# Turning the attention output on the crossbar from batch 2 on, with loads in strict order and more staging

## The chip, the cores and the metric

The kernel runs on one core of one Trainium2 chip. The metric is the device time of one execution in microseconds (us), as the median of several runs of the whole program. Runs are marked fast or slow by their time against the fastest of the same kernel.

Some words that return: in this kernel **TensorE** (PE in the profile) multiplies, **VectorE** (DVE) and **ScalarE** (ACT) work on what it leaves in the memory PSUM, **GpSimd** (POOL) does casts and masks, and **SyncE** (SP) does little but issue DMA transfers (copies between memories). The plan gives each engine one list of instructions. `SPq` in a profile line is SyncE's queue: the time from the start of a DMA-issuing instruction to the moment when the next one may follow. "Crossbar" is here the transpose that a DMA does on its way from SBUF, the on-chip memory, to SBUF.

## The reference, cut to what matters

```
# q, k, v: (8 batches, 8 heads, 576 rows, 64), float32
scores = q @ k^T / 8
scores = where(row // 64 >= column // 64, scores, -1e9)     # block-causal
a = softmax(scores) @ v
x = a.transpose(0, 2, 1, 3).reshape(8*576, 8*64)             # 4608 x 512
h = x @ w_in                                                # 512 -> 2048
out = (h / (1 + exp(-beta * h))) @ w_out                     # 2048 -> 512
```

The feed-forward part needs x with its 512 features on the partitions, so the output of every head pair must be transposed (turned) once: 576 rows of 128 features become 128 partitions of 576 columns. With 8 batches of 4 pairs there are 32 such turns. Q and K of every pair are turned too, to feed the scores.

## The kernel before

The program is first planned and then emitted. Every operation is given to a list scheduler with an assumed length, its dependences, its buffer slots and a priority; the scheduler fixes one order for each of the five engines, and this order is what runs.

```
def schedule(self):                     # cut
    ...
    for e in engs:                      # PE, ACT, DVE, POOL, SP
        if eng_free[e] > now + 1e-9: continue
        for o in pool:                  # operations whose inputs are ready
            ...
            k = (o.prio, o.idx) if e in ("PE",) else (o.prio, o.ready, o.idx)
            ...
        start = now
        eng_free[e] = start + o.dur     # o.dur: the assumed length
        order[e].append(o)              # this order is emitted as it stands
```

Q and K of batches 2 to 7 come in groups of five loads on SyncE (two pairs at a time), are cast to bf16 on GpSimd, and are turned on the crossbar, again by SyncE (cut):

```
z = [g.dma_start(ST[ts.slot][:, i, :, :], src[b, h, 128*i:128*i+128, :]...) for i in range(4)]
z.append(g.dma_start(ST[ts.slot][0:64, 4, :, :], src[b, h, 512:576, :]...))
ld[nm, u] = ld[nm, u + 1] = P.op("SP", 5 * 400, fl, deps=szero, tiles=[ts], xfer=3200, prio=u, ...)
...
def ft(g, e, ...):
    return [g.dma_start_transpose(dst[td.slot][:].rearrange("c (t n) -> c t n", n=128),
                                  nat[tn.slot][:, 0:640])]
cps[nm] = P.op("SP", 1000, ft, deps=[o], tiles=[td, tn], xfer=1500, prio=-1, ...)
```

V comes in six loads per batch, also on SyncE, with a priority that lets it run far ahead; the stores of the result are SyncE's as well. After the attention product and its normalization into the tile xq, TensorE turns the pair and VectorE copies it to x^T, which is kept whole:

```
NE = 3                                  # slots of the exp tiles E
NS = 5                                  # staging slots ST
xq = [sb(f"xq{i}", [128, 5, 128], bf16) for i in range(2)]
xT = sb("xT", [128, 4, NROWS], bf16)    # 4608 columns
...
def fx(g, e, tx=tx, px=px):
    for i in range(5):
        r = 128 if i < 4 else 64
        z = g.transpose(PSb[:, px.slot, 128*i:128*i+r], xq[tx.slot][0:r, i, :], identB[0:r, 0:r])
    return z
xp = P.op("PE", 5 * 57, fx, deps=nrm, tiles=[tx, px], ...)
def fy(g, e, px=px, c=c, b=b):
    return g.tensor_copy(xT[:, c, S*b:S*(b+1)], PSb[:, px.slot, 0:576])
xt.append(P.op("DVE", 425, fy, deps=[xp], tiles=[px], prio=0))
```

The softmax here doesn't subtract the row's maximum and nothing guards it: scores larger than these inputs give would overflow.

## Time and profile before

| what | kernel before |
|---|---|
| median of 4 runs | 389.77 us (389.38 to 391.21) |
| profiled span, mean granted TensorE clock | 389.1 us, 0.947 |
| TensorE / VectorE / ScalarE / GpSimd busy | 349.6 / 168.4 / 209.4 / 96.6 us |
| turns of the attention output on TensorE | 160 instructions (32 pairs of 5) |
| crossbar transposes | 48 (Q and K of 24 pairs) |
| end of the last K transpose on SyncE's queue | 268.3 us |
| feed-forward matmuls after the last attention product | 460 |

These are the busy digits of the page of the kernel before: the span is cut into 40 equal slices (9.7 us each), a digit is the busy share in tenths, and in PEclk it is the granted TensorE clock in tenths.

```profile
PE   3875969999895789999999999999999999999986
PEclk9985779999999569999999999999999999999999
DMA  7989979897998799698967798413001102002002
```

After the uneven first six slices the reader is to see one dent in the PE row, slices 13 to 15 (the hole at 119 to 143 us, with the clock down to 0.5), nearly full digits from then on, and DMA engines that are heavily used until some 240 us and then nearly free. The last attention product runs at 284 us; from there to the end it is feed-forward work alone.

### The profile page before, as it was taken

The numbers are of one execution on the slowest core, as the hardware profiler recorded it, in microseconds if no ns is written. First come the engines' busy times: TensorE is split into PE (matmuls) and PEld (weight loads), VectorE is DVE, ScalarE is ACT, GpSimd is POOL, SyncE is SP. The second block draws the span as 40 slices with busy tenths as digits, with TensorE's granted clock in tenths as the row PEclk, the third lists the DMA queues.
The fourth block names the chain that finished last, engine by engine and source line by source line (L and its number), as shares of the span: only waits on it lengthen the run. The fifth ranks groups of instructions, "written<-read, shape, count | busy, mean of one in ns | idle before, by whom it ended". The sixth has DMA issues, their size and how long they took to land.

```text
span 389.1 us, 6936 instructions
## 1 busy us (share of the span) xinstructions
PE 349.6 (90%) x2709; PEld 176.3 (45%) x2753; DVE 168.4 (43%) x347; ACT 209.4 (54%) x306; POOL 96.6 (25%) x204
## 2 busy tenths in 40 slices
PE   3875969999895789999999999999999999999986
PEld 1552435444452445445545555454554444444432
DVE  5753585217520437413752266512670460550710
ACT  3641648127813458456883788817861551751721
POOL 4390263432202522244153353401100000000000
PEclk9985779999999569999999999999999999999999
DMA  7989979897998799698967798413001102002002
GB/s 173 194 113 229 225 123 180 182 211 168 240 199 176 186 178 199 135 184 205 189 144 167 185 170 144 91 54 89 2 1 56 54 1 83 27 0 83 27 27 81
DMA packets 140384, 50.27 MB, mean 129 GB/s; under 512 B 128560, under 2 KB 135744, under 8 KB 140352
## 3 DMA queue, kind: packets, MB, share of 16 engines
q1 hardware_dynamic: 135744, 45.64, 54.1%
q0 software_dynamic: 4608, 4.20, 7.3%
q8 instruction: 21, 0.34, 0.4%
q14 instruction: 11, 0.09, 0.1%
HBM read 36.71 MB, written 9.44 MB: 119 GB/s over the span
## 4 chain that ended last, share of the span: by engine, by line
PE 68%; DMA 8%; SPq 8%; ACT 7%; DVE 6%; issue 2%; POOL 0%
PE PS L603 29%; PE PS L627 28%; PE PS L546 5%; ACT E L511 5%; PE PS L504 4%; SPq L396 3%; DMA ST<-in_q_dram 3%; ACT th L611 2%; DVE gT L615 2%; DMA KT<-Kn 2%; PE PS L573 2%; SPq L464 2%; DMA w_in<-in_moe_w_in_dram 1%; SPq L400 1%; DMA out_dram<-ost 1%
## 5 line engine op out<-in xcount | busy, mean ns | idle before, releaser
L603 PE MATMUL PS<-xT,w_in 128*128 128x512 bf16 x550 | 135.3, 394 | 6.6 <-DVE xT L579 2.7
L615 DVE SCALAR_TENSOR_TENSOR gT<-th,PS 128x512 bf16<-128x512 f32 x144 | 97.5, 685 | 91.2 <-ACT th L611 91.0
L627 PE MATMUL PS<-w_out,gT 128*128 128x512 bf16 x558 | 125.1, 379 | 4.4 <-DVE gT L615 2.2
L611 ACT ACTIVATE th<-PS,beta 128x512 f32<-128x512 f32 x144 | 98.0, 698 | 42.3 <-PE PS L603 41.1
L511 ACT ACTIVATE E<-PS 128x1024 bf16<-128x1024 f32 x96 | 94.6, 1035 | 40.1 <-PE PS L504 39.9
L627 PEld LDWEIGHTS PS<-w_out,gT 128*128 128x128 bf16 x576 | 54.9, 98 | 68.4 <-DVE gT L615 3.4
L603 PEld LDWEIGHTS PS<-xT,w_in 128*128 128x128 bf16 x576 | 54.0, 101 | 68.9 <-issue 7.8
L638 ACT ACTIVATE ost<-PS 128x512 f32<-128x512 f32 x33 | 19.7, 597 | 94.0 <-PE PS L627 92.2
L504 PE MATMUL PS<-QT,KT 64*128 64x448 bf16 (+5 forms) x384 | 40.9, 303 | 6.6 <-ACT E L511 3.1
L546 PE MATMUL PS<-Vn,E 128*128 128x65 bf16 x960 | 38.0, 201 | 5.5 <-POOL E L519 3.5
L546 PEld LDWEIGHTS PS<-Vn,E 128*128 128x128 bf16 x960 | 35.3, 102 | 12.7 <-POOL E L519 6.6
L579 DVE COPY xT<-PS 128x576 bf16<-128x576 bf16 x32 | 14.5, 454 | 44.1 <-PE PS L573 44.1
L556 DVE RECIPROCAL inv<-PS 128x5 f32<-128x5 f32 x64 | 8.3, 173 | 55.5 <-PE PS L546 55.1
L517 POOL MEMSET E<- 64x128 bf16 x64 | 13.6, 212 | 64.8 <-ACT E L511 60.7
L504 PEld LDWEIGHTS PS<-QT,KT 64*128 64x128 bf16 (+1 forms) x384 | 14.8, 99 | 31.4 <-issue 10.5
L564 DVE TENSOR_TENSOR xq<-PS,inv 128x320 bf16<-128x320 f32 x64 | 28.5, 486 | 0.0
L410 POOL CAST Vn<-Vs 128x2560 bf16<-128x2560 f32 (+2 forms) x9 | 18.8, 2085 | 24.0 <-DMA Vs<-in_v_dram 22.1
L477 POOL CAST Qn<-ST 128x640 bf16<-128x640 f32 x24 | 17.3, 722 | 29.4 <-DMA QT<-Qn 26.7
L477 POOL CAST Kn<-ST 128x640 bf16<-128x640 f32 x24 | 17.3, 723 | 22.0 <-DMA KT<-Kn 19.4
L519 POOL MEMSET E<- 64x256 bf16 x32 | 10.1, 316 | 43.0 <-ACT E L511 42.5
L573 PE MATMUL PS<-identB,xq 128*128 128x128 bf16 (+1 forms) x160 | 17.5, 224 | 1.5 <-DVE xq L564 1.4
L573 PEld LDWEIGHTS PS<-identB,xq 128*128 128x128 bf16 (+1 forms) x160 | 12.5, 100 | 11.8 <-DVE xq L564 2.1
(31 smaller groups left out, 71.3 us busy)
## 6 DMA issues: line engine op xcount, KB each, us to landing
out_dram<-ost SPq DMA_DIRECT2D x36, 256.0 KB, 2.3
Vs<-in_v_dram SPq DMA_DIRECT2D x28, 256.0 KB, 4.6
ST<-in_q_dram SPq DMA_DIRECT2D x48, 128.0 KB, 2.8
ST<-in_k_dram SPq DMA_DIRECT2D x48, 128.0 KB, 2.7
ST<-in_q_dram SPq DMA_DIRECT2D x8, 288.0 KB, 4.2
ST<-in_k_dram SPq DMA_DIRECT2D x8, 288.0 KB, 4.4
w_in<-in_moe_w_in_dram POOLq DMA_DIRECT2D x16, 128.0 KB, 5.7
w_out<-in_moe_w_out_dram POOLq DMA_DIRECT2D x16, 128.0 KB, 4.3
```

Source lines behind the costliest of these rows:

```text
L410: return g.tensor_copy(Vn[t.slot][:, :, h0:h1, 0:64], Vs[ts.slot][:, :, h0:h1, :])
L477: return g.tensor_copy(nat[tn.slot][:, 0:640].rearrange("p (t h d) -> p t h d", t=5, h=2), ST[ts.slot][:, :, a:a + 2, :])
L504: z = g.matmul(o, KT[tk.slot][r, 128 * t:128 * t + m], QT[tq.slot][r, q0:q1])
L511: return g.activation(E3[te.slot][:, g0, :, :], PS[:, ps.slot:ps.slot + 2, :], ACT.Exp, scale=0.125)
L546: z = g.matmul(o, eblk(te, t, i, h), Vn[Tv.slot][:, t, 2 * c + h, 0:65], start=(t == 0), stop=(t == i))
L564: return g.tensor_tensor(xq[tx.slot][:, :, 64 * w:64 * w + 64], a, x, ALU.mult)
L573: z = g.transpose(PSb[:, px.slot, 128 * i:128 * i + r], xq[tx.slot][0:r, i, :], identB[0:r, 0:r])
L603: z = g.matmul(PS[:, ph.slot, :], w_in[:, c, 128 * j:128 * j + 128], xT[:, c, row:row + RC], start=(c == 0), stop=(c == 3))
L611: return g.activation(th[tt.slot][:], PS[:, ph.slot, :], ACT.Tanh, scale=beta[:, j:j + 1])
L615: return g.scalar_tensor_tensor(out=gT[tg.slot][:, j, :], in0=th[tt.slot][:], scalar=1.0, in1=PS[:, ph.slot, :], op0=ALU.add, op1=ALU.mult)
L627: z = g.matmul(PS[:, po.slot, :], gT[tg.slot][:, j, 128 * w:128 * w + 128], w_out[:, j, :], start=(j == 0), stop=(j == NJ - 1))
L638: return g.activation(ost[to.slot][:], PS[:, po.slot, :], ACT.Copy, scale=0.5)
```

## The change

The intent: TensorE is the bound, so take work off it. For batches 2 to 7 the turn of the attention output goes to the crossbar. The free crossbar has its price in the queue, so the change also puts the loads into strict order of use with a limited backlog, so that V no longer runs ahead of Q and K. It keeps x^T in a ring of 2560 columns instead of 4608, and spends the memory won on staging (7 slots instead of 5) and on exp tiles (4 instead of 3). Some assumed lengths of the plan are raised as well. The core of the diff:

```
-        NE = 3
-        NS = 5
+        NE = 4
+        NS = 7
+        RX = 5 * RC                                  # 2560
-        xT = sb("xT", [128, 4, NROWS], bf16)
+        xT = sb("xT", [128, 4, RX], bf16)
 ...
-                o = ld["V", b, h0] = P.op("SP", 6 * 400, fv, ..., prio=... 4 * b + 0.5 - 3 * (b > 1), ...)
+                o = ld["V", b, h0] = P.op("SP", 3000 + 2200 * n, fv, ..., prio=... 4 * b + 0.5, ...)
 ...
+        def pieces(b):                               # split at 512 rows, and where the ring wraps
+            z = []
+            for t0, n in ((0, 512), (512, 64)):
+                x0 = (S * b + t0) % RX
+                m = min(n, RX - x0)
+                z.append((t0, m, x0))
+                if m < n:
+                    z.append((t0 + m, n - m, 0))
+            return z
 ...
-  ... P.op("SP", 5 * 400, fl, ...)
+  ... P.op("SP", 5 * 570, fl, ...)
-  cps[nm] = P.op("SP", 1000, ft, ..., xfer=1500, ...)
+  cps[nm] = P.op("SP", 1280, ft, ..., xfer=800, ...)
 ...
+            if b >= 2:
+                def fy(g, e, tx=tx, c=c, b=b):
+                    z = []
+                    for t0, n, x0 in pieces(b):
+                        ...
+                        z.append(g.dma_start_transpose(xT[:, c, x0:x0+n].rearrange("c (t n) -> c t n", n=m), i))
+                    return z
+                n = len(pieces(b))
+                xt.append(P.op("SP", 400 + 300 * n + 700, fy, deps=nrm, tiles=[tx], xfer=1100, prio=-1, ...))
+                continue
 ...
+        for x, y in zip(seq, seq[1:]):               # seq: all loads of Q, K and V in order of use
+            y.after = x
+        for o in seq:
+            o.lazy = True                            # no load while the assumed backlog is over 4 us
 ...
+            # a crossbar turn into a slot of the ring waits for the matmuls that read it (hs)
+                        xt[4 * b + c].deps += hs
```

A turn is two DMA instructions for most batches and three where the ring wraps (batch 4): 52 for 24 pairs. The plan assumes 1.7 us for a turn of two.

## The prediction

> **What bounds the kernel now.** I read in this order: the table of stretches (busy time and clock), the waits, the chain, the groups, the issuing queue in order of time. The stretches (after the times: each engine's busy us with instructions, granted TensorE clock, DMA share, GB/s):
>
> ```profile
> 28.00:44.00 16.00, 11.91 (x70) 5.56 (x72) 6.55 (x13) 3.44 (x5) 2.68 (x4) 0.57 1.14 224
> 44.00:62.00 18.00, 14.92 (x105) 6.59 (x106) 12.81 (x22) 11.70 (x18) 10.52 (x22) 0.81 0.91 161
> 62.00:119.00 57.00, 53.75 (x440) 27.03 (x444) 22.52 (x51) 26.45 (x39) 14.46 (x24) 1.00 0.94 197
> 119.00:143.00 24.00, 15.91 (x155) 9.12 (x155) 6.32 (x17) 10.53 (x15) 9.50 (x17) 0.64 0.82 190
> 143.00:289.00 146.00, 141.07 (x1317) 74.32 (x1339) 69.76 (x160) 101.80 (x151) 43.54 (x92) 1.00 0.67 132
> ```
>
> The first engine column is TensorE. From 143 us on it works 141 of 146 us at full clock: **TensorE bounds most of the kernel**, so an instruction taken off it there is time saved. Two stretches are different: up to 62 us the DMA engines are full (share 0.9 to 1.1) and TensorE waits at a reduced clock; and 119 to 143 is a hole, with 8 us idle and clock 0.64. The chain of waits says what made the hole:
>
> ```profile
> 118.56 0.63 SPq L467 DMA_DIRECT2D ST<-in_k_dram  x1
> 119.24 1.29 SPq L483 DMA_TRANSPOSE KT<-Kn  x1
> 120.58 2.23 SPq L464 DMA_DIRECT2D ST<-in_q_dram  x4
> 122.85 0.62 SPq L467 DMA_DIRECT2D ST<-in_q_dram  x1
> 123.52 1.30 SPq L483 DMA_TRANSPOSE QT<-Qn  x1
> 124.86 1.28 SPq L483 DMA_TRANSPOSE KT<-Kn  x1
> ```
>
> These are lines of the SyncE queue's time order. The queue issues without a gap from 62 to 126 us; TensorE waits for K transposes that stand behind loads for later use (V of batches 3, 4 and 5 went out ahead of Q and K of batches 2 and 3). The groups that matter:
>
> ```profile
> L573 PE MATMUL PS<-identB,xq 128*128 128x128 bf16 (+1 forms) x160 | 17.5, 224 | 1.5 <-DVE xq L564 1.4
> L579 DVE COPY xT<-PS 128x576 bf16<-128x576 bf16 x32 | 14.5, 454 | 44.1 <-PE PS L573 44.1
> QT<-Qn SPq DMA_TRANSPOSE x24, 2.9
> KT<-Kn SPq DMA_TRANSPOSE x24, 2.7
> ```
>
> The first two are what the change replaces for 24 of 32 head pairs, the last two what it adds more of: 48 crossbar transposes exist, each 2.7 to 2.9 us from issue to landing.
>
> **What the Trainium skill says.** "TensorE: Matmul & The Clock Gate", Part 4, says a TensorE transpose goes to PSUM and needs a copy after it; the trace agrees (L573, then L579). Its Part 1 says the array falls to half clock after about 3.4 us of idleness and needs as long a busy stretch to recover; here the 5 us windows hold 0.50 between 30 and 40 us, and 3 us windows 0.50 from 127 to 142 us, after scattered short waits. "DMA: Bandwidth & Descriptors", "Issuing engine by pattern", allows a transpose only from SyncE or ScalarE; here all are SyncE's, so new ones join the queue that made the hole. "VectorE: DVE Perf Modes", "The three transpose paths", gives 390 ns on TensorE against 1309 ns by crossbar for 128x128. The trace is kinder to both: 224 ns of overlapped busy time, and 2.8 us to land five blocks.
>
> **Part by part.**
>
> TensorE and VectorE. 24 pairs lose 5 transposes each. Their price is not 5 x 224 ns, as they overlap: in the time order the start of such a group lies 0.32 to 0.45 us before the start of the next, so 24 x 0.39 = **9.4 us off TensorE**. VectorE loses 24 x 0.45 = 11 us of copies; it is 43% busy, so this gives nothing by itself. Eight early copies are split in two pieces by the ring; small.
>
> The hole. With loads in strict order, Q and K of the first pairs of batch 2 and then V go first, and V of batch 3 comes after Q of the second pairs. In 119 to 143 TensorE does three attention products, four score groups, two transposes and 7 matmuls: about 9 us at full clock. So **up to 14 us** can be had.
>
> Early part. w_in and w_out are gated as before. The order lets 16 instead of 8 matmuls of the first chunk run before the next Q transpose, and drops a 3.9 us wait of the queue for a staging slot; but with four E buffers the w_out issues on GpSimd now stand behind the masks of two later pairs. I take 2 us gained on TensorE (first chunk done at 84 instead of 86) and the first batch-2 load at 64 instead of 62.
>
> Issuing queue. Durations from its rows, with gaps: a group of five Q or K loads 2.93 us (2.23 + 0.62 + gaps), the six V loads 4.96 (3.12 + 1.77), a crossbar transpose 1.32 (1.28). The x^T turn of a pair is two instructions, 512 and 64 columns (three where the ring wraps), 576 instead of 640 columns: 1.2 us if time goes with columns, 1.7 if half of the 1.28 is fixed per instruction. I take 1.45, an estimate. From the first batch-2 load to the last K transpose: 24 x 2.93 = 70, 6 x 4.96 = 30, 48 x 1.32 = 63, some 20 stores x 0.6 = 12, 21 new turns x 1.45 = 31: **206 us**, against 172 of the same kinds before, where the queue took 62 to 268 and so was idle or held for 32 us of it.
>
> DMA engines. From 242 to 250 us little but transposes run, at shares 0.64 and 0.48: about 0.75 us of all 16 engines each. 24 x 0.7 = 17 us more in a stretch where the share falls from about 0.9: it fits, with no room to spare.
>
> The sum. In the changed order of instructions 616 feed-forward matmuls and 24 pairs stand between the end of the first chunk and the last attention product, then 408 matmuls. A matmul costs 0.22 us (448 in 98.5 us from 287.4 to 385.9), a pair without its turn 2.05 (attention product 0.95 to 1.0, twelve score matmuls 1.05). If TensorE never waits: 84 + 616 x 0.22 + 24 x 2.05 = 269, + 408 x 0.22 = 359, + 3 to the end = **362**. If the queue sets the pace: 64 + 206 + 3 (stores of the first chunk hold it once) = 273 for the last K; the K of the second last pair, which the order asks for first, lands at about 274; then 48 matmuls and two pairs, 15 us, + 90 + 3 = **382**. Per pair the queue needs 206/24 = 8.6 us and TensorE 185/24 = 7.7, so after using up its lead the queue is the slower one. I expect many waits of 1 to 5 us in place of one hole of 14.
>
> **Rivals.** (a) The queue keeps up, because turns are cheap (1.2) or its lead covers: 362 to 370. For it: the changed schedule was made with longer issue times, so its order allows for them. Against: the queue was already full from 62 to 126. (b) The queue is the new bound, near 380: the sum above. (c) The two hold each other up: a turn waits at the queue's head for VectorE, the Q and K transposes behind it come late, TensorE idles and drops to half clock: 388 and more. For it: one in-order queue, two xq buffers, and clock 0.50 after only 1 to 2 us waits in the hole. Against: in the order a turn stands after later pairs' Q or K transposes, and four E buffers loosen it. (d) The turns leave TensorE but the end doesn't move, as the last 100 us are feed-forward alone: no, since fewer matmuls are left after the last attention product (408, not 460).
>
> **Range and chances.** Between (a) and (b), closer to (b): 379. Turn cost 1.2 to 1.7 moves the end by 5 us each way, queue waits of 10 us add up to 10; so 366 to 391. The 2% line is 382.2, just above the point: faster 0.58, same 0.38, slower 0.04.
>
> **What would show it.** L573 with 40 instead of 160 instructions, and 24 fewer xT copies (not counting split ones); the 119 to 143 hole gone; new x^T rows among the DMA issues, on SyncE 1.2 to 1.7 us a pair; the queue issuing almost without gaps from 64 to 270; TensorE waits for KT and QT of several us each between 140 and 280 under (b), none under (a), and clock below 1 there under (c). Last attention product at about 270 under (a), 290 under (b). I am wrong if an x^T turn issues in much more or less than 1.45 us, if loads issue faster with more staging, or if a feed-forward wait for xT grows.

## The result, and the profile after

The changed kernel is **slower**: 424.51 us (423.3 to 427.08, 4 runs) against 389.77 us. The ratio is 1.0893, with a 95% interval of 1.083 to 1.0955. Here and below a ratio is the mean time of one kernel's fast runs over the mean of the other's fast runs of the same rounds, so it is not quite the ratio of the medians that are quoted. The result is correct, and the profiled run is one with a span of 425.3 us and a mean clock of 0.932.

First the same digits of the page of the changed kernel (a slice is 10.6 us):

```profile
PE   3768989996979777959776869698759999999987
PEclk9986989999799988998995989979989999999999
DMA  6799789997797785847935695659750200101102
```

There is no longer one deep dent. Instead the PE row shows digits from five to eight, in between nines, all the way to 319 us. The DMA row is not higher than before, which speaks against the transfers themselves as what is short. In the stretches that the prediction used (PE, PEld, DVE, ACT and POOL with busy us and instructions, then clock, DMA share, GB/s), the kernel after stands so:

```profile
62.00:119.00 57.00, 51.74 (x417) 24.76 (x414) 21.12 (x52) 29.32 (x44) 17.51 (x35) 0.94 0.93 174
119.00:143.00 24.00, 18.34 (x175) 9.40 (x173) 7.89 (x19) 12.22 (x18) 6.92 (x12) 1.00 0.81 160
143.00:289.00 146.00, 117.71 (x907) 54.23 (x909) 42.62 (x94) 74.39 (x109) 36.29 (x71) 0.89 0.67 143
```

In 119 to 143 us TensorE does more than before (175 instructions against 155, at full clock against 0.64): the hole is gone. But in the next 146 us it is busy for 117.7 us where it was busy for 141.1, and does 907 instructions where it did 1317. What it waits for is in the list of waits (engine, line, what for: us in total, times, longest). First the kernel before, whose score matmuls stand in line 504, then the kernel after, where they stand in line 526:

```profile
PE PS L504 <- DMA KT<-Kn: 2.0, 1, 2.0
```

```profile
PE PS L526 <- DMA KT<-Kn: 34.1, 15, 4.5
PE PS L568 <- DMA xT<-xq: 5.8, 2, 3.1
PE PS L568 <- POOL E L541: 4.9, 3, 2.4
```

One 2 us wait for a turned K has become 15 waits with 34 us. None is longer than 4.5 us. They lie in the stretch of 100 to 320 us. What stands before a late K is seen in the time order of SyncE's queue, here around the wait that ended at 143 us (start, us, line, what, how many). L486 and L489 load Q and K, L505 turns Q and K, L598 is the new turn of the attention output, L704 stores a result:

```profile
139.80 2.88 SPq L505 DMA_TRANSPOSE KT<-Kn  x2
142.73 2.53 SPq L598 DMA_TRANSPOSE xT<-xq  x2
145.30 1.27 SPq L505 DMA_TRANSPOSE QT<-Qn  x1
146.62 0.58 SPq L704 DMA_DIRECT2D out_dram<-ost  x1
147.25 2.14 SPq L486 DMA_DIRECT2D ST<-in_k_dram  x4
149.44 0.63 SPq L489 DMA_DIRECT2D ST<-in_k_dram  x1
150.16 1.24 SPq L505 DMA_TRANSPOSE QT<-Qn  x1
151.45 2.53 SPq L598 DMA_TRANSPOSE xT<-xq  x2
```

The queue is full: each line starts some 0.05 us after the end of the one before. It goes on like this from 66.0 us to the end of the last K transpose at 316.0 us; the gaps between lines are 5.6 us in all. A turn of one pair is two instructions and 2.53 us. Another turn happens to fall apart into two lines when the view is cut between them; the first piece has 512 columns, the second 64:

```profile
127.58 1.29 SPq L598 DMA_TRANSPOSE xT<-xq  x1
128.92 1.22 SPq L598 DMA_TRANSPOSE xT<-xq  x1
```

An eighth of the columns takes 0.07 us less. So on the queue the cost goes with the **instruction**, and hardly with its size. The sums of the queue's lines from 66.0 to 316.0 us, in us, beside the prediction's terms:

| on SyncE's queue | predicted | measured |
|---|---|---|
| loads of Q and K | 70 | 72.7 |
| loads of V | 30 | 32.2 |
| transposes of Q and K (48) | 63 | 66.2 |
| stores (20) | 12 | 12.2 |
| turns of the attention output (21 pairs, 46 instructions) | 31 | 61.1 |
| gaps and holds | 3 | 5.6 |
| sum | 209 | 250.0 |

TensorE has lost its turns as intended: 40 instead of 160 instructions. This is worth nothing here, as TensorE is no longer what the kernel waits for.

### The profile page after: what moved, and what is told of

Same layout as the page of the kernel before. It is cut to its first block, busy times and chain, and to the rows that moved or that the text cites. A ratio compares the mean times of both kernels' runs of the same rounds, so it can differ in the third digit from the quotient of the medians.

```text
span 425.3 us, 6777 instructions
## 1 busy us (share of the span) xinstructions
PE 356.4 (84%) x2633; PEld 168.6 (40%) x2633; DVE 160.3 (38%) x331; ACT 211.3 (50%) x308; POOL 97.0 (23%) x205
## 3 DMA queue, kind: packets, MB, share of 16 engines
q0 software_dynamic: 4608, 4.20, 6.9%
## 5 line engine op out<-in xcount | busy, mean ns | idle before, releaser
L656 PE MATMUL PS<-xT,w_in 128*128 128x512 bf16 x576 | 142.5, 400 | 2.1 <-DVE xT L617 1.2
L687 PE MATMUL PS<-w_out,gT 128*128 128x512 bf16 x576 | 135.2, 393 | 3.2 <-DVE gT L670 3.2
L687 PEld LDWEIGHTS PS<-w_out,gT 128*128 128x128 bf16 x576 | 56.3, 101 | 75.0 <-issue 11.1
L526 PE MATMUL PS<-QT,KT 64*128 64x448 bf16 (+5 forms) x384 | 42.2, 310 | 38.6 <-DMA KT<-Kn 34.1
L698 ACT ACTIVATE ost<-PS 128x512 f32<-128x512 f32 x35 | 20.9, 597 | 96.7 <-PE PS L687 96.7
L568 PE MATMUL PS<-Vn,E 128*128 128x65 bf16 x960 | 36.9, 199 | 11.2 <-DMA xT<-xq 5.8
L568 PEld LDWEIGHTS PS<-Vn,E 128*128 128x128 bf16 x960 | 34.2, 101 | 20.1 <-issue 8.4
L541 POOL MEMSET E<- 64x256 bf16 x32 | 10.2, 319 | 35.6 <-ACT E L533 34.4
L467 PE MATMUL PS<-identB,Qn 96*128 96x96 bf16 x48 | 4.4, 242 | 8.4 <-POOL Vn L364 4.6
L393 POOL DMA_DIRECT2D w_out<-in_moe_w_out_dram x16 | 8.7, 563 | 0.3 <-POOL E L539 0.3
L388 POOL DMA_DIRECT2D w_in<-in_moe_w_in_dram x16 | 8.7, 563 | 0.1
```

The costliest lines, as they stand in the source:

```text
L526: z = g.matmul(o, KT[tk.slot][r, 128 * t:128 * t + m], QT[tq.slot][r, q0:q1])
L568: z = g.matmul(o, eblk(te, t, i, h), Vn[Tv.slot][:, t, 2 * c + h, 0:65], start=(t == 0), stop=(t == i))
L656: z = g.matmul(PS[:, ph.slot, :], w_in[:, c, 128 * j:128 * j + 128], xT[:, c, row % RX:row % RX + RC], start=(c == 0), stop=(c == 3))
L687: z = g.matmul(PS[:, po.slot, :], gT[tg.slot][:, j, 128 * w:128 * w + 128], w_out[:, j, :], start=(j == 0), stop=(j == NJ - 1))
L698: return g.activation(ost[to.slot][:], PS[:, po.slot, :], ACT.Copy, scale=0.5)
```

## The experiments

Fifteen kernels were run, each beside the kernel before on the same chip. The theories at the start:

- **Q**: SyncE's queue sets the pace, and a turn costs it some 1.2 us *per instruction*.
- **D**: the transfers set the pace (bytes of transposes on the DMA engines), whatever the number of instructions.
- **P**: the fixed order is at fault, planned with turns of 1.7 us where they take 2.5.
- Later **N**: any new plan of this kernel costs about 2%, whatever it is planned from.

The expectations below are quoted. The letters in them are mostly these.

### The turn: how many instructions

**Three instructions per pair.** The 512 columns are cut in two halves of 256: 72 instructions instead of 52, and not a byte more. The planned lengths were left, so the order on TensorE, ScalarE, VectorE and GpSimd is the same as in the changed kernel (checked instruction by instruction).

```
+ z += [(t0, 256, x0), (t0 + 256, 256, x0 + 256)] if n == 512 else [(t0, n, x0)]
```

> The changed kernel in the same planned order, each pair turned by three instructions of 256, 256 and 64 columns; 72 instead of 52 transpose instructions, same bytes. Theory Q: 20 x 1.25 = 25 us more queue time, time 445 to 452. Theory D: 425, unchanged.

Measured: 447.62 us, ratio 1.1466 (1.1416 to 1.1517); the last K transpose ends at 336.4 us.

**One instruction per pair.** Again the same order, but the turn moves 640 columns (the last 64 are not needed and are overwritten later) in one instruction, two where the ring wraps: 28 in all, and 11% *more* bytes.

```
+ def turns(b):
+     x0 = S * b % RX
+     if x0 + 640 <= RX: return [(0, 640, x0)]
+     return [(0, RX - x0, x0), (RX - x0, 640 - (RX - x0), 0)]
```

> The changed kernel in the same planned order, but each pair is turned by one instruction of 640 columns (the last 64 columns are waste that the next batch overwrites) instead of two of 512 and 64; only batch 4, where the ring wraps, keeps two. 28 to 32 of 52 transposes go, bytes rise by about a tenth. Theory Q (a fixed 1.25 us per instruction): 24 of 52 instructions go, 30 us less queue time, time 390 to 400. Theory D (the transposes cost by bytes, in the DMA engines or the crossbar): 425 or a little more.

Measured: 396.71 us, ratio 1.0161 (1.0128 to 1.0195); the last K transpose ends at 286.3 us.

With 28, 52 and 72 instructions the times are 396.7, 424.5 and 447.6 us: 1.16 us for every instruction between the two far points, and on a straight line (52 would lie at 424.5). The waits of TensorE for K follow, first in the kernel with one instruction per pair, then in that with three:

```profile
PE PS L532 <- DMA KT<-Kn: 18.7, 13, 4.2
```

```profile
PE PS L532 <- DMA KT<-Kn: 41.0, 13, 7.0
```

As the order of all other engines and the bytes are the same (with 28 even more bytes), theory D falls, and the larger part of the loss belongs to Q. What is left at one instruction, 1.6%, needs another cause.

**The turn alone.** The kernel before with nothing but the crossbar turn (two instructions, no ring, its own order of loads):

```
+ if b >= 2:
+     def fy(...): return [g.dma_start_transpose(xT[... 512 columns], xq[...]),
+                          g.dma_start_transpose(xT[... 64 columns], xq[...])]
+     xt.append(P.op("SP", 400 + 300 * 2 + 700, fy, deps=nrm, ...)); continue
```

> The kernel before with only the crossbar turn added (two instructions a pair from batch 2 on), old load order, full x^T, 5 staging buffers, 3 E buffers. Theory Q: the queue needs 172 us of issues plus 60 for the turns, so the time is 415 to 435, as bad as the full change or worse. Theory S: near 390.

Measured: 419.21 us, ratio 1.0738 (1.0685 to 1.0792). The queue has no gap from 61.6 to about 320 us, and the last K transpose ends at 299.4 us, 31 us later than before. The turns need about 60 us; the rest fits the some 30 us in which the queue had been idle or held. So the turn costs over 7% by itself.

**The turn undone.** The changed kernel with `if b >= B` in place of `if b >= 2`: order, ring and staging stay, TensorE turns.

> The changed kernel with only the crossbar turn undone: all 32 pairs are turned on TensorE again; strict load order, backlog, ring and staging stay, and the schedule is planned anew. Theory Q (the SyncE issuing queue is the new bound, because each crossbar transpose holds it for about 1.25 us whatever its size): 52 instructions, 66 us, leave the queue; from the first batch-2 load to the last K transpose it needs about 190 us instead of 250, TensorE sets the pace again, and the time is 370 to 385. Theory S (the strict load order or the backlog limit makes loads late): stays above 405.

Measured: 397.66 us, ratio 1.0189 (1.0139 to 1.0239); last K transpose at 273.4 us. A miss: I had hoped for a gain, and the parts that were to help cost 1.9%. The next three runs look into that.

### Order and staging

**Order only**: the kernel before with the strict order, the limited backlog and the new assumed lengths, nothing else.

```
+ y.after = x ... o.lazy = True ; lengths 3000+2200n, 5*570, 1280 as in the change
```

> The kernel before with only the load order changed: strict order of use, backlog limit, V no longer ahead, the new planned lengths; old staging, full x^T, turn on TensorE. The 1.9% that the changed kernel loses with its turn on TensorE comes from the order or from the staging. If the order costs it: 394 to 400; if the staging: 384 to 391.

Measured: 397.41 us, ratio 1.0245 (1.0181 to 1.0309). The stretch of 120 to 140 us (columns as above) of the kernel before, then the same and the next stretch of this kernel, then the two waits of this kernel's TensorE that grew:

```profile
120.00:140.00 20.00, 11.97 (x113) 6.75 (x114) 4.45 (x13) 9.60 (x13) 9.50 (x17) 0.63 0.78 184
```

```profile
120.00:140.00 20.00, 16.50 (x186) 8.73 (x186) 7.99 (x20) 14.55 (x21) 6.64 (x16) 1.00 1.02 203
140.00:160.00 20.00, 16.19 (x185) 9.09 (x185) 11.82 (x29) 13.80 (x21) 8.56 (x15) 1.00 0.84 165
```

```profile
PE PS L512 <- DMA KT<-Kn: 11.5, 7, 3.7
PE PS L554 <- POOL E L527: 11.4, 7, 3.2
```

The hole is filled, as predicted (186 instructions instead of 113, full clock). But 11.5 us of waits for K and 11.4 us for the masks of GpSimd have come up, spread over 100 to 180 and 220 to 260 us, where the kernel before had 2.0 and 3.5 us in all. In 140 to 160 us TensorE is busy for 16.2 us instead of 19.0.

**Staging only**: the kernel before with 7 staging slots, 4 exp tiles and the ring (and its dependences).

```
+ NE, NS, RX = 4, 7, 5 * RC        # V keeps its old priority, no strict order, TensorE turns
```

> The kernel before with only 7 staging buffers, 4 E buffers and the x^T ring, old load order and planned lengths, turn on TensorE. If the staging costs the 1.9% (the w_out issues on GpSimd stand behind masks of later pairs): 393 to 400; if the order does: 384 to 391.

Measured: 398.74 us, ratio 1.0249 (1.0198 to 1.03). First the stretch of 120 to 140 us, then the wait of TensorE that empties it, then the stretch of SyncE's queue ahead of it (L486 and L489 load Q and K, L406 and L410 load V, L505 turns Q and K):

```profile
120.00:140.00 20.00, 8.15 (x89) 4.85 (x89) 2.69 (x10) 6.54 (x9) 4.86 (x12) 0.53 0.91 198
```

```profile
PE PS L526 <- DMA KT<-Kn: 10.9, 2, 10.5
```

```profile
116.45 1.31 SPq L505 DMA_TRANSPOSE QT<-Qn  x1
...
118.43 2.13 SPq L486 DMA_DIRECT2D ST<-in_k_dram  x4
120.60 0.63 SPq L489 DMA_DIRECT2D ST<-in_k_dram  x1
121.27 3.58 SPq L406 DMA_DIRECT2D Vs<-in_v_dram  x4
124.89 1.75 SPq L410 DMA_DIRECT2D Vs<-in_v_dram  x2
126.69 1.30 SPq L505 DMA_TRANSPOSE KT<-Kn  x1
```

The hole has become deeper (8.15 us busy instead of 11.97), with one wait of 10.5 us for a K. Between the Q transpose and the K transpose that goes with it, five loads of K and six of V for later use are issued, so K comes 10.2 us after Q; in the kernel before the same two transposes start at 114.95 and 119.24 us. With more room to run ahead, more loads stood ahead of what TensorE needed next. Slots, exp tiles and ring were changed together here and are not told apart.

**Only another plan.** Both parts change the plan; perhaps any other plan costs 2%? The kernel before with another slack on TensorE in the scheduler, and nothing else:

```
- SLACK = 120.0
+ SLACK = 150.0
```

> The kernel before with one planning constant changed (the slack that the planner gives TensorE, 120 to 150 ns): the same instructions, buffers and loads, another order. It measures what a new plan alone is worth. Theory N (the kernel before is a well-picked plan, and any new plan costs about 2%, so the 1.9 to 2.5% of the three runs without a crossbar turn says nothing against strict order or staging): 394 to 402. Theory S (order and staging themselves cost 2%): 387 to 392.

Measured: 392.12 us, ratio 1.004 (0.9993 to 1.0087). One sample is not a proof (the control with deeper buffers below, 1.0024, is a second), but it speaks against N: order and staging have a cost of their own, about 2% each, and together (the run with the turn undone) 1.9%, so the two do not add up.

### The plan's lengths

**True lengths.** The changed kernel with one number of the plan set to what the trace shows:

```
- xt.append(P.op("SP", 400 + 300 * n + 700, fy, ...
+ xt.append(P.op("SP", 1290 * n, fy, ...
```

> The changed kernel with nothing but the planned length of a turn raised from 1.7 (2.0) us to 1.29 us per instruction, so that the schedule knows what the trace shows. Theory Q: the same instructions stand in the queue, in another order; 415 to 428. Theory P (the fixed order was planned with too short a turn, and TensorE waits for that reason): 398 to 410.

Measured: 407.39 us, ratio 1.0475 (1.0419 to 1.0532), 17 us less than the changed kernel. The last K transpose ends at 317.4 us, as late as before (316.0). What changed is TensorE's order: 320 feed-forward matmuls stand after the last attention product instead of 408. A matmul takes 0.215 us (93 in a stretch of 20 us of the kernel with the order alone, where nothing but feed-forward work is left), so 88 of them are 18.9 us, and the span fell by 425.3 − 406.0 = 19.3 us. The queue is as slow as it was, but TensorE has more work to do while it would wait. Its waits for K:

```profile
PE PS L526 <- DMA KT<-Kn: 17.6, 9, 4.2
```

These are 17.6 us in 9 waits, against 34.1 us in 15. P was right about the time and Q about the queue. Both hold: the queue sets when the last pair can run, and the plan sets how much is left to do after it.

### Relieving the queue

If SyncE's queue is the bound, other issues can move to ScalarE's queue. I left the transposes on SyncE: the Trainium skill, "DMA: Bandwidth & Descriptors", section "Silent corruption: two transposing streams in flight at once", warns that transposes issued from two queues can corrupt each other unless one waits for the other. No run here tried it.

**V on ScalarE.** The changed kernel with the V loads of batches 2 to 7 issued by ScalarE, one by one and without a place in the strict order:

```
- o = ld["V", b, h0] = P.op("SP", 3000 + 2200 * n, fv, ...)
+ vs.append(P.op("ACT", 800, fv1, ...))        # six per batch
```

> The changed kernel with the V loads of batches 2 to 7 (36 DMAs, about 33 us of issuing) issued by ScalarE's queue instead of SyncE's; the same bytes, packets and crossbar transposes, planned anew. Theory Q (SyncE's issuing queue is the bound): 25 to 33 us go, 392 to 402. Theory D (DMA engines or the crossbar themselves are the bound, wherever a DMA is issued from): 420 or more.

Measured: 425.23 us, ratio 1.0934 (1.0872 to 1.0995): no gain, a miss. The trace says why this one doesn't answer the question. The lines are ScalarE's time order:

```profile
64.75 4.83 ACTq L421 DMA_DIRECT2D Vs<-in_v_dram  x3
...
87.17 0.69 ACT L678 ACTIVATE th<-PS,beta 128x512 f32<-128x512 f32 x1 [21.42 <-issue]
```

Most of the V of three batches went out in one burst from 64 to 87 us, and ScalarE did no arithmetic for 21.4 us: here the DMA issues were not free for the engine that made them. The last K transpose still ended earlier, at 306.7 us instead of 316.0.

**V on ScalarE, in order, true lengths.** As the run with true lengths, and V by ScalarE with its place in the strict order.

```
+ P.op("SP", 1290 * n, fy, ...)                        # the turn's true length
+ vs.append(P.op("ACT", 800, fv1, ..., prio=-1, ...))  # V, six per batch
+ seq += [ld["V", b, 2 if b == 0 else 0]] if b < 2 else ld["V", b, 0]
```

> The run with true turn lengths (two instructions a pair) plus the V loads of batches 2 to 7 on ScalarE's queue, this time in the strict order of use, so that they cannot run ahead. What to read is the end of the last K transpose, 317 us without the move. In all nine runs so far with V on SyncE or not, the span was that end + 0.2145 us for each feed-forward matmul ordered after the last attention product + 20. Theory Q (issuing queue): 33 us of issues leave, last K transpose ends at 282 to 292, time 400 to 410 (456 matmuls are ordered after, against 320). Theory D (DMA engines or crossbar): last K transpose at 310 or later, time 428 or more.

Measured: 413.49 us, ratio 1.0621 (1.0517 to 1.0725). The last K transpose ends at 293.8 us, 23.6 us earlier than in the run with true lengths alone, for some 32 us of issues removed. But the plan, which sees a lighter queue, left 456 feed-forward matmuls after the last attention product, not 320: 136 x 0.215 = 29 us more at the end. 29.2 − 23.6 = 5.6, and the measured difference of the two medians is 6.1 us.

**One instruction per turn, true lengths, and V on ScalarE in order** (the last edit, with `turns(b)` in place of `pieces(b)`):

```
+ xt.append(P.op("SP", 1290 * len(turns(b)), fy, ...))
```

> One turn instruction of 640 columns a pair, true planned lengths, V loads in order on ScalarE's queue: the relief of both parts together. Theory Q: last K transpose 286 - 33 = 253 to 260, 452 matmuls after it, 370 to 380: faster than the kernel before. Theory D: no better than 394.

Measured: 405.27 us, ratio 1.0432 (1.0342 to 1.0521). **The same, with the stores instead of V on ScalarE**:

```
- P.op("SP", 400, fd, deps=[x], tiles=[to], xfer=900, ...)
+ P.op("ACT", 400, fd, deps=[x], tiles=[to], xfer=900, ...)
```

> One turn instruction of 640 columns a pair, true planned lengths, and the output stores (not the V loads) on ScalarE's queue, 16 us of issues less. Theory Q: last K transpose at 268 to 275, 444 matmuls after it, 382 to 390. Theory D: 394 or more.

Measured: 401.18 us, ratio 1.0299 (1.0235 to 1.0364). Both are misses; the last K transpose ends at 282.8 and 281.9 us, hardly earlier than with one turn alone (286.3). And the plan left 452 and 444 matmuls for the end instead of 408, which is 9.5 and 7.7 us more; so with the turn's true length, here shorter than the planned 1.7 us, and with the moved issues, these two kernels came out slower than the one with one turn alone (396.7). The queue is lighter, but now it is held at its head. These are some of the queue's own waits in the run with V on ScalarE, from the list of waits cut to 60 to 283 us, that is to the last K transpose (L523 is the transposes of Q and K, L557 and L559 the masks of GpSimd, L724 the stores, L616 the turn):

```profile
SPq L523 <- POOL E L557: 12.5, 11, 3.1
SPq L523 <- POOL E L559: 8.9, 8, 3.9
SPq L724 <- ACT ost L718: 7.5, 3, 3.1
SPq L616 <- DVE xq L604: 5.8, 5, 2.1
```

A wait at the head keeps everything behind it waiting; a part of such a wait overlaps the issue itself. Put together, the queue was not issuing for 29.1 of the 218.4 us of this stretch, against 11.9 of 221.9 us with one turn alone, and its loads of K took 43.8 us instead of 34.4. The list for the whole run also has a wait of a turn for xq of 10.4 us, but it ends at 297 us, after the last K transpose, so it delayed no K.

**Deeper buffers.** Are these waits a matter of slots? The kernel with one instruction per turn, true lengths and V on ScalarE, now with deeper buffers:

```
- NS = 7 ; Qn, Kn: 2 slots ; QT, KT: 3 slots ; xq: 2 slots
+ NS = 6 ; Qn, Kn: 3 slots ; QT, KT: 4 slots ; xq: 3 slots
```

> The run with one turn a pair, true lengths and V on ScalarE's queue (405), with 4 QT and KT, 3 Qn and Kn, 3 xq buffers and 6 instead of 7 staging buffers. There the queue's transposes waited about 60 us at its head for casts, masks, score matmuls and normalised tiles. Theory C (mutual waiting through too few slots): those waits halve, last K transpose at 255 to 270, 375 to 390. Otherwise 400 to 408.

Measured: 408.17 us, ratio 1.0438 (1.038 to 1.0495). The last K transpose moves up to 270.3 us, but the time doesn't fall, and the waits of the transposes for the masks are 19.3 us, as against 21.4. (The turn waits 15.3 us for xq in the whole run, 12.6 of them after the last K.) As a control, **the kernel before with 4 slots of QT and KT and 3 of xq**:

```
- QT, KT: 3 slots ; xq: 2 slots
+ QT, KT: 4 slots ; xq: 3 slots
```

> The kernel before with 4 instead of 3 QT and KT buffers and 3 instead of 2 xq buffers, nothing else. Theory C (Q and K transposes wait at the head of the issuing queue for a QT or KT slot that TensorE has to free, 12 us there, and hold the loads behind them): the waits of transposes on TensorE fall below 4 us and the time is 380 to 388. If slots don't matter: 387 to 400, as any new plan.

Measured: 391.31 us, ratio 1.0024 (0.9982 to 1.0066), though its last K transpose ends at 248.2 instead of 268.3 us. In the kernel before, the transposes wait for TensorE (13.4 us among the queue's own waits) more than TensorE for them (2.0 us); so there the end of the last K transpose is a consequence, and in the changed kernel it is a cause.

**The lightest queue.** TensorE turns (as in the run with the turn undone), V on ScalarE in order, and the deeper buffers:

```
- if b >= 2:                      # the crossbar turn
+ if b >= B:
+ vs.append(P.op("ACT", 800, fv1, ..., prio=-1, ...))
+ NS = 6 ; Qn, Kn: 3 slots ; QT, KT: 4 slots ; xq: 3 slots
```

> New order and staging, turn on TensorE, V on ScalarE's queue in order, 4 QT and KT, 3 Qn and Kn, 3 xq, 6 staging buffers: the lightest SyncE queue of all, about 157 us of issues. If the queue or its slots hold the rest up: 376 to 386, faster than the kernel before. If plans and waits elsewhere do: 390 to 400.

Measured: 390.41 us (387.68 to 396.24, one run of four slow and left out), ratio 1.0001 (0.9936 to 1.0065). It wins back the 1.9% of that run and no more. It changes V and buffers at once, so which of them did it is not told apart. No version beats the kernel before.

### What the runs say together

| kernel | turn instructions on SyncE | end of last K transpose, us | feed-forward matmuls after the last attention product | span, us | span − K − 0.215 x matmuls |
|---|---|---|---|---|---|
| before | 0 | 268.3 | 460 | 389.1 | 22 |
| turn undone | 0 | 273.4 | 468 | 395.7 | 22 |
| one per pair | 28 | 286.3 | 408 | 394.1 | 20 |
| **after** | 52 | 316.0 | 408 | 425.3 | 22 |
| three per pair | 72 | 336.4 | 408 | 445.6 | 22 |
| true lengths | 52 | 317.4 | 320 | 406.0 | 20 |
| true lengths, V on ScalarE | 52 | 293.8 | 456 | 410.5 | 19 |

The last column is the last pair's own work and the end; it hardly moves (22 to 25 in the runs without deeper slots that are not listed). So the time of the changed kernel is made of two things: when the queue is done with the last K, and how many matmuls the plan has kept for later. In the runs with deeper QT and KT slots the column is 37 to 44, as the K transposes can then run ahead, and their end no longer says when the last pair runs.

**What stays open**: why taking issues away from the queue gives less than these issues took (some 32 us of V moved the last K by 24 us with two instructions per turn, and by 3.5 us with one). With V on ScalarE and one instruction per turn, the waits at the queue's head for the masks grew from 5.6 us (one turn alone, up to the last K) to 21.4, and deeper slots left 19.3; with the stores moved instead they were 5.2 us, and K was hardly earlier either. Whether it is the order on GpSimd or the assumed lengths of the plan, no run here tells. Open too is whether the 1.2 us of an instruction is the queue's own work or a wait for the crossbar behind it: no run issued a turn from another queue.

## Why the prediction was wrong, point by point

**The bound.** That the queue would take the place of TensorE was rival (b), and it is what happened: full from 66 to 316 us, with "many waits of 1 to 5 us in place of one hole of 14". The size was wrong.

**The failed step is the term "21 new turns x 1.45 = 31"** in the sum of the issuing queue. It measured 61.1 us for the turns of the same stretch (46 instructions, 1.33 us each on average). Both ends of the bracket were mistaken: "1.2 us if time goes with columns" and "1.7 if half of the 1.28 is fixed" leave out the third case, that all of the 1.28 is fixed, and that one makes 2.56 us for two instructions. It is what the runs showed (1.29 us for 512 columns, 1.22 us for 64, and 1.16 us of total time for each one added or removed). A pair costs 2.5 us. The profile before held a hint. The prediction's own lines show four Q loads of 128 partitions in 2.23 us and then one of 64 partitions in 0.62 us: half the bytes, no less time. (A slip that changes nothing: its 172 us for the kernel before are 175 by its own terms.)

**The other terms of the queue** were each a little short (loads, V and transposes by 8 us together, gaps by 3, the start by 2). With the 30 us of the turns this makes the 43 us by which the last K transpose was late: 316.0 us, predicted 273. So with the turn priced right the sum would have been 382 + 30 = 412 us, still 12 us low. In the run with one instruction per turn, the turns take about what the prediction assumed; there K ends at 286.3 us and the time is 396.7 us, past the top of the range (391) too.

**From the last K to the end** the prediction had 1 + 15 + 90 + 3 = 109 us. Measured: 425.3 − 316.0 = 109.3 us. The last attention product, expected at 290 us under (b), starts at 331.4 us, which is the same delay of some 40 us. This half of the sum was right, so the whole miss is in when K comes.

**The hole.** Predicted: gone, worth up to 14 us. It is gone, but in the run with the order alone nothing is won: waits come back, spread out. I took the removal of a wait for the removal of its cause; that the cause is the queue's total work, which had not become less, is argued and not shown. The reading of the hole was also too narrow: of the 8 us that TensorE is idle in it, one wait of 2.0 us is for a K transpose, and the others, 0.5 to 1.9 us each, are put down to exp tiles, masks and VectorE.

**The early part.** "2 us gained" was not seen: the first load of batch 2 starts at 66.0 us, not 64, and the staging that was to help costs 2% by itself.

**TensorE's 9.4 us.** The count was right (160 to 40 instructions). It was the gain that the change was made for, and it went where TensorE waits anyway.

**DMA engines.** "It fits" was right: their share in the three stretches is 0.93, 0.81 and 0.67, where it was 0.94, 0.82 and 0.67, and theory D fell with the run that moved more bytes in fewer instructions.

**Rival (c), half clock.** In part: 0.89 from 143 to 289 us, where it had been 1.00, but the worst stretch of 20 us has 0.74 (220 to 240 us), and the clock is mostly low where the waits for K are. The turn's wait at the queue's head, which was (c)'s argument, was small in the changed kernel (4.1 us for xq, none over 1.0), and the long ones of the lightened queue came after the last K.

**The plan's lengths.** The prediction took comfort in a schedule "made with longer issue times, so its order allows for them". For the turns it wasn't: 1.7 us planned, 2.5 taken, and this alone is 17 us of the loss.

## What to carry to other kernels

Before moving work to a DMA, count instructions on the queue that must issue them, one by one, and set their sum for a unit of work against the time that the busiest engine needs for the same unit. Here a transfer that was split in two for a small remainder paid twice, and one instruction with some bytes too many was cheaper by 28 us. And where an order is fixed by a plan, look at what its assumed lengths leave for the end: a wrong one on a single kind of operation cost 17 us here. Measured lengths alone are no guarantee: in the runs with a lightened queue the plan, made with them, left more work for the end (444 to 456 matmuls), not less.

## What the Trainium skill lacked or had wrong

- "DMA: Bandwidth & Descriptors" gives no figure for trn2 by name for how long a transpose from SBUF to SBUF occupies the queue that issues it. Here it is 1.29 us for 512 columns and 1.22 us for 64 (median of all 52: 1.236 us; of 28 with 640 columns: 1.276 us).
- The same page, "Issuing engines are not separate DMA queues", calls the sequencer's time for a DMA "usually small relative to the DMA itself". In this case it was the bound: a turn's instruction held the queue for 1.24 us of the 2.4 us to its landing (medians), the queue was full for 250 us, from 100 us on at DMA shares of 0.55 to 0.78, and one added instruction cost 1.16 us of total time.
- The same section doesn't say what the issues cost the engine that takes them over. Here V loads issued from ScalarE kept it from arithmetic for 21.4 us.
- "Advanced Engine Details and Errata", "X-Bar Transpose (TRN2)", says that transposes are as fast as regular DMAs. In landing they are (2.4 to 2.7 us here, a Q load 2.8 us); in issuing they are not: 1.24 us against 0.51 (128 partitions) and 0.63 us (64) for a load of Q or K (medians).
- "VectorE: DVE Perf Modes", "The three transpose paths", has 1309 ns for one 128x128 block on the crossbar. Here turns of 512 columns, four such blocks, landed in 2.5 us and those of the remaining 64 columns in 2.4 us (medians), so the time to landing did not go with the number of blocks.
